# Two decodings of w_in put behind the row maxima on VectorE

## The chip, the cores and the metric

The kernel runs on one core of a Trainium2 chip. A core has five engines that share one on-chip memory and synchronise by semaphores: TensorE (PE, matmuls and transposes), VectorE (DVE), ScalarE (ACT), GpSimd (POOL) and SyncE (SP, which issues nearly all DMA transfers of this kernel). Each engine takes its instructions strictly in the order in which they stand in its own list. The metric is the device time of one execution in microseconds (us). Before the change it is 562.74 us, the median of 3 runs (561.09 to 566.05).

## What is computed

```python
# attention with decay, 4 batches x 8 heads, 576 tokens, head size 64
scores = q @ k.T / 8 + (cum[:, None] - cum[None, :])    # cum: running sum of log f; causal
attn   = softmax(scores);  y = attn @ v                 # -> x: 2304 x 512
# a gated layer
h = x @ w_in                                            # 512 x 2048
x = (h * sigmoid(1.702 * h)) @ w_out                    # 2048 x 512
# soft mixture of 8 experts with 4 slots each
logits = x @ phi                                        # 2304 x 32
slots  = softmax(logits, over tokens).T @ x             # 32 x 512
slots  = relu(slots @ w1[e]) @ w2[e]                    # 8 experts, 512 x 1024 x 512
out    = softmax(logits, over slots) @ slots            # 2304 x 512
```

`w_in` and `w_out` arrive as 64-bit floating point numbers. No engine computes in that format, so the kernel builds the 32-bit value of each element out of the two 32-bit halves of its words. That is the decoding that the change moves.

## The kernel before

**Attention.** The 2304 tokens are taken in 20 rows of up to 128 tokens, five for each batch (the fifth has 64). `prep_row` splits a row's queries and keys into a coarse and a fine 16-bit part and brings them into transposed form: for rows 0 to 2 by PE transposes whose results DVE and ACT copy out of PSUM, from row 3 on by transposing DMAs on SP's queue. For rows 1 to 4 the subtraction that makes the fine part stands on POOL (L325, L329), else on DVE. For rows 0 to 4 the row maximum is found ahead of the exponentials: `emit_max` computes the scores a first time (tile `scm`, in PSUM) and reduces them on DVE (L387) into tile `mt`; row 1 has 4 such steps of two heads each (u = 0 to 3) and row 3 has 8 of one head. `emit_mrow` negates the maxima on DVE (L432), PE transposes them (`mT`, L436), and ACT writes them beside the queries (L445), so that the second computation of the scores (tile `scs`, L467 to L471) already has the maximum taken off. Then follow the exponential on ACT (L489) and the product with the values on PE (`pv`, L623). `scm` and `scs` share 3 PSUM buffers: a new one is written only when DVE or ACT has read an old one.

**Decoding w_in.** It has 16 tiles of 128x512. Tile n is decoded in `w_first` in four steps: the word that holds sign, exponent and upper digits is scaled (L208 on POOL for even n, L210 on ACT for odd n), the lower word is converted into tile `low` (L211, ACT), and two DVE instructions join them with shifts and masks (L213 writes `low`, the **first half** below; L216 writes the tile, the **second half**). `low` has 2 buffers; one becomes free when a second half has read it. Then `split_one` makes a coarse part on ACT (L277) and a fine one on POOL (L278) for the matmuls `hp` (L800 to L802). Tiles 0 to 3 serve the first 512 columns of h, tiles 8 to 11 the third. `w_out` is decoded by the same lines later.

**Order.** The program is written in one sequence, in which `more_w` calls put the decoding between attention steps. A scheduler then places the instructions of each engine by its own forecast of when they can start, so that a line may stand earlier or later on its engine than in the program text. `tc.issue_after(x)` holds the instructions under it behind x on their engine; the kernel uses it already for some transposes of the gated layer.

**Later.** From about 46 us the gated layer's matmuls run between attention steps. When the last attention step is done its memory is given back, and the 127 loads of the experts' weights start (`we`, L1051), which the last part of the kernel works on.

Of the kernel before, what the change touches and what calls it, by code (L numbers as in the profile page):

```python
# [15 lines left out]
ALU = mybir.AluOpType  # L16
# [14 lines left out]
def attention_moe_softmoe(ctx, tc, q, k, v, f, w_in, w_out, phi, w1, w2, out):  # L31
    nc = tc.nc
# [28 lines left out]
    def ps_sc(name):  # L61
        return ps.tile([128, 512], F32, tag="sc", name=name, bufs=3)
# [106 lines left out]
    def w32_tile(n):  # L169
        if n < NI:  # L170
            return wp.tile([128, 512], F32, tag=f"w{n + 1}" if n < NI - 1 else "o0", name="w32")
        ff = n - NI
        if ff % 2 == 0:
            wo_pair[ff // 2] = wp.tile([128, 2, 512], F32, tag=f"o{ff // 2}", name="wo")
        return wo_pair[ff // 2][:, ff % 2]
# [21 lines left out]
    def w_first(n):  # L197


        if n in W32:  # L200
            nc.scalar.activation(out=W32[n], in_=W32[n], func=AF.Copy, scale=WS)
            return
        words = w_raw.pop(n).rearrange("p (n w) -> p n w", w=2)
        lo, hi = words[:, :, 0], words[:, :, 1]
        val = W32[n] = w32_tile(n)
        low = ap_.tile([128, 512], U32, tag="low", name="low", bufs=N_LOW)
        if n % 2 < 1:
            nc.gpsimd.tensor_scalar(out=val, in0=hi.bitcast(F32), scalar1=2.0 ** -111, scalar2=None, op0=ALU.mult)  # L208
        else:
            nc.scalar.activation(out=val, in_=hi.bitcast(F32), func=AF.Copy, scale=2.0 ** -111)  # L210
        nc.scalar.activation(out=low, in_=lo, func=AF.Copy, scale=0.93 * 2.0 ** -29)  # L211
        bits = val.bitcast(U32)
        nc.vector.scalar_tensor_tensor(  # L213
            out=low, in0=bits, scalar=3, in1=low, op0=ALU.logical_shift_left, op1=ALU.bitwise_or
        )
        nc.vector.scalar_tensor_tensor(  # L216
            out=bits, in0=bits, scalar=0x80000000, in1=low, op0=ALU.bitwise_and, op1=ALU.bitwise_or
        )

    def more_w(to):  # L220
        while w_at[0] < min(NW, to):
            n = w_at[0]
            w_at[0] += 1
            while w_loaded[0] < min(NW, n + W_AHEAD):
                w_load(w_loaded[0])
                w_loaded[0] += 1
            w_first(n)
            if n < NI:
                split_one(n)
            else:  # L230
                WO[n - NI] = W32.pop(n)
                if w_phi:
                    fold_phi(*w_phi.pop())
                w_phi.append((n - NI,))
        if w_at[0] == NW and w_phi:
            fold_phi(*w_phi.pop())
# [129 lines left out]
    def mask_in(o, m):  # L366
        nc.vector.tensor_tensor(out=o, in0=o, in1=m.unsqueeze(1).to_broadcast(list(o.shape)), op=ALU.add)

    def emit_max(r, u):
        b, i = rows[r]  # L370
        base = ROW[b, 0]
        m = mt[r % 2]
        if rows_of[i] == 128:
            hb = max(1, 4 // (i + 1))
            nb = 128 * (i + 1)
            sc = ps_sc("scm")
            for hh in range(hb):
                h = u * hb + hh
                for j in range(i + 1):
                    o = sc[:, hh * nb + 128 * j:hh * nb + 128 * (j + 1)]  # L380
                    mask = j == i and r < 5
                    nc.tensor.matmul(o, lhsT=QA[r][:, h, :], rhs=KA[base + j][:, h, :], start=True, stop=not mask)
                    if mask:
                        nc.tensor.matmul(o, lhsT=identb, rhs=mqk, start=False, stop=True)
            if r >= 5:
                mask_in(sc[:, 0:hb * nb].rearrange("p (h n) -> p h n", h=hb)[:, :, 128 * i:], mqk)
            nc.vector.tensor_reduce(  # L387
                out=m[:, 96 + u * hb:96 + (u + 1) * hb],
                in_=sc[:, 0:hb * nb].rearrange("p (h n) -> p h n", h=hb), axis=AX.X, op=ALU.max,
            )  # L390
        else:

            n = rows_of[i]
            sc = ps_sc("scm")
            if u < H // 2:
                for j in range(i):
                    for a in range(2):
                        nc.tensor.matmul(
                            sc[64 * a:64 * a + n, 128 * j:128 * (j + 1)], lhsT=QA[r][:, 2 * u + a, 0:n],
                            rhs=KA[base + j][:, 2 * u + a, :], start=True, stop=True,  # L400
                        )
                nc.vector.tensor_reduce(
                    out=m4[:, u], in_=sc[:, 0:128 * i], axis=AX.X, op=ALU.max
                )
            else:
                mask = r < 5
                for u in range(H // 2):
                    for a in range(2):
                        o = sc[64 * a:64 * a + n, n * u:n * (u + 1)]
                        nc.tensor.matmul(  # L410
                            o, lhsT=QA[r][:, 2 * u + a, 0:n], rhs=KA[r][:, 2 * u + a, 0:n], start=True, stop=not mask
                        )
                        if mask:
                            nc.tensor.matmul(o, lhsT=identb[:, 0:n], rhs=mqk[:, 0:n], start=False, stop=True)
                sv = sc[:, 0:n * (H // 2)].rearrange("p (h n) -> p h n", n=n)
                if not mask:
                    for a in range(2):
                        mask_in(sv[64 * a:64 * a + n], mqk[64 * a:64 * a + n, 64 * a:64 * a + n])
                m2 = ap_.tile([128, H // 2, 1], F32, tag="m2", name="m2", bufs=2)
                nc.vector.tensor_reduce(out=m2, in_=sv, axis=AX.X, op=ALU.max)  # L420
                nc.vector.tensor_tensor(out=m4, in0=m4, in1=m2, op=ALU.max)
# [228 lines left out]
    for pair in range(B // 2):  # L650
# [4 lines left out]
        n = rows_of[-1]  # L655
# [22 lines left out]
    def attn_items():  # L678
# [12 lines left out]
        for r in range(len(rows)):  # L691
# [27 lines left out]
            if r >= 1 and not late(r):  # L719
                n_m = n_max(r)  # L720
                hi = b0 - 1.5
                lo = max(preps.get(r, 0.0) + 0.5, hi - 0.9 * n_m)
                hi = max(hi, lo + 0.3)
                for m in range(n_m):
                    add(lo + (hi - lo) * (m + 0.5) / n_m, CM, emit_max, r, m)
                add(max(hi, b0 - 2), CR, emit_mrow, r)
# [337 lines left out]
    if True:  # L1064
# [6 lines left out]
        for u in range(n_max(0)):  # L1071
            emit_max(0, u)
# [18 lines left out]
        n = 0  # L1091
# [10 lines left out]
        for c in range(NCH):  # L1102
            t0, t1 = goals[c], goals[c + 1]
            NSTEP = 2 * N_UNIT
            n = 0
# [59 lines left out]
        for hf in range(2):  # L1165
            hsb[hf] = G[NCH - 1, 1, "ab"[hf]].rearrange("p a n -> p (a n)")
            for n in range(2):
# [9 lines left out]
                if done:  # L1177
                    turn(*done[-1])
                nc.scalar.activation(
                    out=hsb[hf][:, n * 512:(n + 1) * 512], in_=l1, func=AF.Relu, scale=zi[:, hf:hf + 1]  # L1180
# [21 lines left out]
        for p, (c0, c1) in enumerate(PARTS):  # L1202
            w = c1 - c0
            nr = 2
            for fb in range(WHOLE - KE, KE):
# [15 lines left out]
                out=s4[64:128], in0=p4[64:128], scalar=SS, in1=s4[64:128], op0=ALU.mult, op1=ALU.subtract  # L1221
# [13 lines left out]
            for k, blks in enumerate(groups):  # L1235
# [10 lines left out]
                if len(blk_tok[blks[0]]) == 1:  # L1246
                    tok = blk_tok[blks[0]][0][2]
                    queue.dma_start(
                        out=out[tok:tok + 128 * m, c0:c1].rearrange("(t p) n -> p t n", p=128), in_=ob
# [37 lines left out]
```

## Time and profile before

| | before |
|---|---|
| median of 3 runs | 562.74 us (561.09 to 566.05) |
| the profiled execution | 562.1 us, of which the span of its trace 560.4 us |
| mean granted TensorE clock | 0.973 of full speed |
| PE busy | 506.8 us (90%) |
| DVE busy | 354.5 us (63%) |
| ACT busy | 309.2 us (55%) |
| POOL busy | 69.0 us (12%) |

The span runs from the first to the last instruction of the profiled execution; 1.7 us of that execution lie outside of it. A share of busy time is an average over stages: POOL does nearly all of its work in the first 126 us, and DVE is far busier there than later. The time that an engine was idle before an instruction is put down to whatever released that instruction last. Register and semaphore work isn't counted as busy.

### The profile page before, as it was taken

What the parts mean: (1) busy time and instruction counts of PE and PEld (TensorE: products, weight loads), DVE (VectorE), ACT (ScalarE), POOL (GpSimd) and SP (SyncE); (2) the same over time, 40 slices, a digit from 0 to 9 for tenths busy, and PEclk for the clock granted to TensorE, in tenths of its full rate; (3) what the DMA queues carried; (4) which work ended last, traced back from release to release, by engine and by line L of the source; (5) the groups of instructions that cost most, each with busy time, mean ns of one, the idle gap of its engine ahead of it and who ended that gap; (6) DMA issues with size and microseconds to landing.
All of it is one profiled execution on the core that took longest, in us unless ns stands there. A gap on an engine that the chain in (4) does not pass through costs nothing.

```text
span 560.4 us, 13652 instructions
## 1 busy us (share of the span) xinstructions
PE 506.8 (90%) x5387; PEld 317.4 (57%) x5387; DVE 354.5 (63%) x934; ACT 309.2 (55%) x604; POOL 69.0 (12%) x120
## 2 busy tenths in 40 slices
PE   3566999998989999999999799989999999899991
PEld 3455876775666555665665466546566545454431
DVE  8988969787667357577776667866764413352022
ACT  6767786786767354565666566756564233312111
POOL 4866743310000000000000000000000000000000
PEclk9879799998999999999999899999999999999997
DMA  9997674999867227996759979995544199999999
GB/s 241 275 363 173 171 126 151 262 183 190 153 130 121 58 39 146 181 182 99 130 99 151 154 139 155 208 163 104 85 78 79 37 344 369 363 341 338 379 294 284
DMA packets 229823, 105.63 MB, mean 188 GB/s; under 512 B 202592, under 2 KB 211296, under 8 KB 229760
## 3 DMA queue, kind: packets, MB, share of 16 engines
q1 hardware_dynamic: 228528, 103.59, 80.0%
q10 hardware_dynamic: 1232, 1.18, 0.7%
q8 instruction: 42, 0.69, 0.5%
q14 instruction: 21, 0.17, 0.1%
HBM read 64.63 MB, written 4.72 MB: 124 GB/s over the span
## 4 chain that ended last, share of the span: by engine, by line
PE 70%; DMA 12%; DVE 8%; ACT 5%; issue 2%; SPq 2%; ACTq 0%; DVEq 0%
PE hp L800 10%; PE hp L801 9%; PE hp L802 9%; DMA ph<-pn 6%; PE gT L756 5%; PE p L778 4%; PE pv L623 3%; PE pv L628 3%; PE l L1172 3%; PE sp L921 2%; DMA kf<-in_k_dram 2%; PE scs L551 2%; DMA we<-in_moe_w_dram 2%; PE scs L552 2%; PE pv L630 2%
## 5 line engine op out<-in xcount | busy, mean ns | idle before, releaser
L800 PE MATMUL hp<-w,xt 128*128 128x512 f16 x288 | 110.4, 383 | 0.3 <-DVE spart L928 0.3
L801 PE MATMUL hp<-w,xt 128*128 128x512 f16 x288 | 109.8, 381 | 0.0
L802 PE MATMUL hp<-w,xt 128*128 128x512 f16 x288 | 109.7, 381 | 0.0
L578 ACT ACTIVATE pf<-scs,mx 128x512 f32<-128x512 f32 (+3 forms) x108 | 57.6, 541 | 40.9 <-DVE mx L574 31.7
L814 DVE SCALAR_TENSOR_TENSOR g<-g,hp 128x512 f32<-128x512 f32 x72 | 49.2, 683 | 41.6 <-ACT g L813 40.9
L813 ACT ACTIVATE g<-hp 128x512 f32<-128x512 f32 x72 | 42.6, 591 | 51.6 <-PE hp L802 46.4
L587 DVE SCALAR_TENSOR_TENSOR pn<-pf,pn 128x512 f16<-128x512 f32 (+2 forms) x78 | 51.0, 657 | 31.0 <-ACT pn L586 30.4
L586 ACT ACTIVATE pn<-pf 128x512 f16<-128x512 f32 (+2 forms) x78 | 47.0, 606 | 26.3 <-DMA ph<-pn 25.0
L628 PE MATMUL pv<-vv,ph 128*128 128x65 f16 (+2 forms) x360 | 45.9, 199 | 7.9 <-DMA ph<-pn 7.7
L574 DVE CUSTOM_DVE_ANT_0 scs<-scs,zmq 128x128 f32<-128x128 f32 (+3 forms) x96 | 46.6, 495 | 9.1 <-PE scs L552 6.9
L802 PEld LDWEIGHTS <-xt 128*128 128x128 f16 x288 | 28.3, 98 | 33.3 <-issue 0.6
L763 ACT COPY gt<-gT 128x512 f32<-128x512 f32 x71 | 41.1, 583 | 9.7 <-PE gT L756 9.3
L628 PEld LDWEIGHTS <-ph 128*128 128x128 f16 (+2 forms) x360 | 34.4, 102 | 20.0 <-DMA ph<-pn 10.2
L629 PE MATMUL pv<-vv,ph 128*128 128x65 f16 (+2 forms) x360 | 45.3, 196 | 0.0
L756 PE MATMUL gT<-ident,g 128*128 128x128 f32 x288 | 45.1, 277 | 0.0
L630 PE MATMUL pv<-vv,ph 128*128 128x65 f16 (+2 forms) x360 | 45.1, 195 | 0.0
L800 PEld LDWEIGHTS <-xt 128*128 128x128 f16 x288 | 28.8, 100 | 27.8 <-issue 4.7
L756 PEld LDWEIGHTS gT<-ident,g 128*128 128x128 f32 x288 | 33.9, 142 | 14.4 <-issue 5.0
L801 PEld LDWEIGHTS <-xt 128*128 128x128 f16 x288 | 28.3, 98 | 22.7 <-issue 0.7
L629 PEld LDWEIGHTS <-ph 128*128 128x128 f16 (+2 forms) x360 | 34.7, 103 | 1.9 <-issue 0.2
L551 PE MATMUL scs<-kab,qa 128*128 128x128 f16 x240 | 35.2, 220 | 0.4 <-ACT pf L578 0.4
L585 POOL MEMSET pn<- 128x128 f16 x12 | 2.5, 210 | 267.3 <-DMA ph<-pn 165.8
(226 smaller groups left out, 1036.3 us busy)
## 6 DMA issues: line engine op xcount, KB each, us to landing
we<-in_moe_w_dram SPq DMA_DIRECT2D x127, 256.0 KB, 5.6
raw<-in_moe_w_in_dram SPq DMA_DIRECT2D x16, 512.0 KB, 7.3
raw<-in_moe_w_out_dram SPq DMA_DIRECT2D x16, 512.0 KB, 6.0
kf<-in_k_dram SPq DMA_DIRECT2D x13, 256.0 KB, 3.7
qf<-in_q_dram SPq DMA_DIRECT2D x13, 256.0 KB, 4.1
vf<-in_v_dram SPq DMA_DIRECT2D x12, 256.0 KB, 4.4
out_dram<-ob SPq DMA_DIRECT2D x12, 256.0 KB, 3.2
ph<-pn SPq DMA_TRANSPOSE x78, 3.3
```

The costliest lines, as they stand in the source:

```text
L574: nc.vector.tensor_tensor_reduce(out=o, in0=o, in1=mask, scale=-SC, scalar=3.0e38 if n == 128 else DG[r][1][:, u], op0=ALU.add, op1=ALU.mi ...
L578: nc.scalar.activation(out=pf[:, hh * nb:(hh + 1) * nb], in_=o, func=AF.Exp, bias=mx[:, hh:hh + 1], scale=-1.0)
L586: nc.scalar.activation(out=pn[:, 0, 0:w], in_=pf, func=AF.Copy, scale=PB)
L587: nc.vector.scalar_tensor_tensor(out=pn[:, 1, 0:w], in0=pf, scalar=PB, in1=pn[:, 0, 0:w], op0=ALU.mult, op1=ALU.subtract)
L628: nc.tensor.matmul(o, lhsT=ph[0:rr, 0, off:off + n], rhs=vh, start=(j == 0), stop=False)
L629: nc.tensor.matmul(o, lhsT=ph[0:rr, 0, off:off + n], rhs=vl, start=False, stop=False)
L630: nc.tensor.matmul(o, lhsT=ph[0:rr, 1, off:off + n], rhs=vh, start=False, stop=(j == i))
L756: last_turn[0] = nc.tensor.transpose((pt if a < 2 else pt2)[:, a * 128:(a + 1) * 128], g[:, a * 128:(a + 1) * 128], ident)
L800: nc.tensor.matmul(hp, lhsT=xt[:, 0, kk, ts], rhs=win(0, fg, kk), start=(kk == 0), stop=False)
L801: nc.tensor.matmul(hp, lhsT=xt[:, 0, kk, ts], rhs=win(1, fg, kk), start=False, stop=False)
L802: last_hp[0] = nc.tensor.matmul(hp, lhsT=xt[:, 1, kk, ts], rhs=win(0, fg, kk), start=False, stop=(kk == KD - 1))
L814: nc.vector.scalar_tensor_tensor(out=g, in0=g, scalar=1.0, in1=hp, op0=ALU.add, op1=ALU.mult)
```

## The change

The first half of tile 2 is held behind the maximum (row 1, u = 3) on DVE, and the first half of tile 9 behind the maximum (row 3, u = 1). `maxima` keeps the reductions by row and step, so that they can be named. No instruction is added or taken away.

```diff
         bits = val.bitcast(U32)
-        nc.vector.scalar_tensor_tensor(
-            out=low, in0=bits, scalar=3, in1=low, op0=ALU.logical_shift_left, op1=ALU.bitwise_or
-        )
+        with tc.issue_after(maxima[BEHIND[n]].ins) if n in BEHIND else nullcontext():
+            nc.vector.scalar_tensor_tensor(
+                out=low, in0=bits, scalar=3, in1=low, op0=ALU.logical_shift_left, op1=ALU.bitwise_or
+            )
...
+    maxima = {}
+    BEHIND = {2: (1, 3), 9: (3, 1)}
...
-            nc.vector.tensor_reduce(
+            maxima[r, u] = nc.vector.tensor_reduce(
```

Since four lines are added, later lines of the changed kernel have higher numbers: L213 and L216 become L214 and L217, and from L217 on four are added (L387 becomes L391, L432 becomes L436).

**DVE, around row 1's maxima.** `w_222`, `w_233`, `w_371`, `w_405`, `w_500`, `w_545` are tiles 0 to 5 of w_in; `mt_84` holds the maxima of row 1. Before:

```order
L216 SCALAR_TENSOR_TENSOR w_233<-w_233,low 128x512
L213 SCALAR_TENSOR_TENSOR low<-w_371,low 128x512
L387 TENSOR_REDUCE mt_84<-scm 128x2 x2
L216 SCALAR_TENSOR_TENSOR w_371<-w_371,low 128x512
L213 SCALAR_TENSOR_TENSOR low<-w_405,low 128x512
L387 TENSOR_REDUCE mt_84<-scm 128x2
L216 SCALAR_TENSOR_TENSOR w_405<-w_405,low 128x512
L637 TENSOR_SCALAR rd<-pv 128x4
L213 SCALAR_TENSOR_TENSOR low<-w_500,low 128x512
L387 TENSOR_REDUCE mt_84<-scm 128x2
...
L213 SCALAR_TENSOR_TENSOR low<-w_545,low 128x512
L432 TENSOR_SCALAR mt_84<-mt_84 128x8
```

And now:

```order
L217 SCALAR_TENSOR_TENSOR w_233<-w_233,low 128x512
L391 TENSOR_REDUCE mt_84<-scm 128x2 x2
L214 SCALAR_TENSOR_TENSOR low<-w_405,low 128x512
L391 TENSOR_REDUCE mt_84<-scm 128x2
L217 SCALAR_TENSOR_TENSOR w_405<-w_405,low 128x512
L391 TENSOR_REDUCE mt_84<-scm 128x2
L214 SCALAR_TENSOR_TENSOR low<-w_371,low 128x512
L436 TENSOR_SCALAR mt_84<-mt_84 128x8
L641 TENSOR_SCALAR rd<-pv 128x4
L214 SCALAR_TENSOR_TENSOR low<-w_500,low 128x512
L217 SCALAR_TENSOR_TENSOR w_371<-w_371,low 128x512
```

Tile 2 stands behind the four maxima. Tile 3, which isn't held, has moved ahead of it, between the maxima. Three halves stand between tile 1 and the negation where seven stood.

**DVE, around row 3's first maxima.** `w_849`, `w_936`, `w_947`, `w_958`, `w_969` are tiles 7 to 11; `mt_83` holds the maxima of row 2 and `mt_84` those of row 3. Before:

```order
L432 TENSOR_SCALAR mt_83<-mt_83 128x8
L213 SCALAR_TENSOR_TENSOR low<-w_849,low 128x512
...
L216 SCALAR_TENSOR_TENSOR w_936<-w_936,low 128x512
L213 SCALAR_TENSOR_TENSOR low<-w_947,low 128x512
L814 SCALAR_TENSOR_TENSOR g<-g,hp 128x512
L637 TENSOR_SCALAR rd<-pv 128x4
L216 SCALAR_TENSOR_TENSOR w_947<-w_947,low 128x512
L213 SCALAR_TENSOR_TENSOR low<-w_958,low 128x512
...
L216 SCALAR_TENSOR_TENSOR w_969<-w_969,low 128x512
L323 COPY kan<-cpart 64x8x3
L387 TENSOR_REDUCE mt_84<-scm 128x1 x2
```

And now:

```order
L214 SCALAR_TENSOR_TENSOR low<-w_849,low 128x512
L436 TENSOR_SCALAR mt_83<-mt_83 128x8
...
L217 SCALAR_TENSOR_TENSOR w_936<-w_936,low 128x512
L641 TENSOR_SCALAR rd<-pv 128x4
L214 SCALAR_TENSOR_TENSOR low<-w_958,low 128x512
...
L214 SCALAR_TENSOR_TENSOR low<-w_969,low 128x512
L217 SCALAR_TENSOR_TENSOR w_969<-w_969,low 128x512
L391 TENSOR_REDUCE mt_84<-scm 128x1 x2
L214 SCALAR_TENSOR_TENSOR low<-w_947,low 128x512
```

Tile 9 stands behind row 3's first two maxima; tiles 10 and 11 still stand ahead of them. A half of tile 7 has moved ahead of row 2's negation.

**ACT, from row 1's negation to row 2's queries.** `qa<-mT` is the copy of the negated maxima, `qbn<-kqf` the coarse part of row 2's queries. Before:

```order
L211 ACTIVATE low<-raw 128x512
L277 ACTIVATE w<-w_371 128x512
L211 ACTIVATE low<-raw 128x512
L318 ACTIVATE kbn<-kqf 128x8x64
L489 ACTIVATE pf<-scs 128x512
L211 ACTIVATE low<-raw 128x512
L321 ACTIVATE qbn<-kqf 128x8x64
L277 ACTIVATE w<-w_405 128x512
L445 ACTIVATE qa<-mT 8x1024
```

And now:

```order
L211 ACTIVATE low<-raw 128x512
L322 ACTIVATE kbn<-kqf 128x8x64
L493 ACTIVATE pf<-scs 128x512
L449 ACTIVATE qa<-mT 8x1024
L281 ACTIVATE w<-w_371 128x512
L211 ACTIVATE low<-raw 128x512 x2
L325 ACTIVATE qbn<-kqf 128x8x64
L281 ACTIVATE w<-w_405 128x512
```

The copy of the maxima has moved ahead of tile 2's split, two conversions and row 2's queries. Behind these places the scheduler's order differs on every engine to the end of the attention; PE's own order is the same past the second group of `hp` matmuls, up to row 3's last maxima, but for one group of four `pv` products.

## Rows read from the trace of the kernel before

**Rows 1.** The page: busy tenths and granted clock in 40 slices of 14 us.

```profile
PE   3566999998989999999999799989999999899991
DVE  8988969787667357577776667866764413352022
PEclk9879799998999999999999899999999999999997
```

**Rows 2.** Timeline of PE: start us, duration us, what; in brackets the idle time before.

```profile
30.47 0.46 PE L436 MATMUL mT<-ident,mt 128*104 128x128 f32 x1 [6.85 <-DVE mt L432]
...
33.69 1.06 PE L340 MATMUL kqT<-ident,qbn 128*128 128x128 f16 x8
...
50.69 0.22 PE L384 MATMUL scm<-zmq,identb 128*128 128x128 bf16 x1
56.46 0.27 PE L467 MATMUL scs<-qa,kab 128*128 128x128 f16 x1 [5.55 <-DVE mt L387]
```

**Rows 3.** Windows of PE: from:to, length, busy us (count), granted clock, DMA.

```profile
35.00:36.50 1.50, 1.50 (x21) 0.94 0.99 322
...
54.50:56.00 1.50, 0.00 (x0) 0.88 0.67 268
...
62.00:63.50 1.50, 1.50 (x11) 0.84 0.76 147
```

**Rows 4.** Timeline of DVE around the maxima of rows 1 and 3.

```profile
18.76 0.69 DVE L216 SCALAR_TENSOR_TENSOR w<-w,low 128x512 uint32<-128x512 uint32 x1
...
22.74 1.64 DVE L213 SCALAR_TENSOR_TENSOR low<-w,low 128x512 uint32<-128x512 uint32 x1
24.31 0.68 DVE L387 TENSOR_REDUCE mt<-scm 128x2 f32<-128x512 f32 x1
24.91 0.68 DVE L216 SCALAR_TENSOR_TENSOR w<-w,low 128x512 uint32<-128x512 uint32 x1
...
29.30 1.12 DVE L432 TENSOR_SCALAR mt<-mt 128x8 f32<-128x8 f32 x1
...
45.69 0.17 DVE L432 TENSOR_SCALAR mt<-mt 128x8 f32<-128x8 f32 x1
...
49.78 1.20 DVE L213 SCALAR_TENSOR_TENSOR low<-w,low 128x512 uint32<-128x512 uint32 x1 [1.12 <-ACT low L211]
...
51.50 0.15 DVE L637 TENSOR_SCALAR rd<-pv 128x4 f32<-128x4 f32 x1
...
55.73 1.27 DVE L387 TENSOR_REDUCE mt<-scm 128x1 f32<-128x512 f32 x2
...
57.29 3.35 DVE L328 COPY qan<-qbn 64x512 f16<-64x512 f16 x1
```

**Rows 5.** Timeline of POOL beside the two long DVE instructions.

```profile
22.37 1.46 POOL L278 TENSOR_TENSOR w<-w,w 128x512 f16<-128x512 f32 x1
...
57.04 1.20 POOL L325 TENSOR_TENSOR kbn<-kf,kbn 64x512 f16<-64x512 f32 x1
58.21 1.14 POOL L329 TENSOR_TENSOR qbn<-qf,qbn 64x512 f16<-64x512 f32 x1
59.32 1.14 POOL L278 TENSOR_TENSOR w<-w,w 128x512 f16<-128x512 f32 x1
```

**Rows 6.** Windows: busy us (count) of PE, PEld, DVE, ACT, POOL; clock, DMA.

```profile
14.00:98.00 84.00, 65.69 (x647) 52.92 (x644) 74.96 (x135) 60.27 (x105) 51.30 (x42) 0.90 0.78 210
98.00:448.00 350.00, 338.29 (x3771) 212.03 (x3769) 236.30 (x681) 214.25 (x433) 10.84 (x45) 0.99 0.76 133
448.00:504.00 56.00, 53.92 (x432) 27.80 (x434) 19.61 (x60) 15.57 (x36) 0.68 (x1) 1.00 1.00 356
```

**Rows 7.** Timeline of SP's queue: the first stretch of the expert loads.

```profile
445.77 23.89 SPq L1051 DMA_DIRECT2D we<-in_moe_w_dram  x35
```

**Rows 8.** Timeline of PE and ACT: a later `hp`, and row 2's queries.

```profile
84.58 0.38 PE L800 MATMUL hp<-w,xt 128*128 128x512 f16 x1
...
28.41 0.62 ACT L321 ACTIVATE qbn<-kqf 128x512 f16<-128x512 f32 x1
```

## Prediction

> **What bounds the kernel now.** I began with the slices [rows 1]. PE is at 9 tenths nearly everywhere from the fifth slice on, so past 56 us a microsecond is won only by starting PE's work earlier. Before that PE stands at 5 and 6 tenths while DVE is at 8 and 9, and the granted clock dips in the third and fifth slice. The windows say it in sums [rows 6]: from 14 to 98 us PE works 65.7 of 84 us and DVE 75.0; from 98 to 448 us PE leaves only 11.7 of 350 us unused. So DVE bounds the start, and PE the rest up to 448 us. The end hangs on the same clock: the first of the experts' loads goes out at 445.77 us, when the last attention step has given its memory back [rows 7], and from then on the DMA engines are at 1.00 [rows 6]. What comes after that point keeps its length, so a gain that lasts until 446 us counts in full at the end.
>
> Then PE's timeline [rows 2]. Two idle stretches stand out: 6.85 us until row 1's negated maxima come (30.47), and 5.55 us until row 3's first maximum frees a PSUM buffer (56.46). These are the two places that the change touches. After each the clock is at half for a while [rows 3]: the window at 35.0 still has 0.94; the one at 54.5 has 0.88, which puts the fall at about 55.6, and the one at 62.0 has 0.84, which puts the return at about 62.5. PE thus worked at half speed from 56.46 to 62.5, 6.0 us that full speed would do in 3.0.
>
> Last DVE's own timeline [rows 4]. A maximum and a decoding half follow each other at 0.60 us (24.31 to 24.91). Some take longer because POOL is at work: the half at 22.74 lasts 1.64 beside a POOL subtraction from 22.37 to 23.83 [rows 4, 5], which is 0.96 over the usual 0.68; the negation at 29.30 takes 1.12 for eight columns.
>
> **The change part by part.** Nothing is added or removed; DVE has the same instructions in another order.
>
> Row 1. Tile 1's second half ends at 18.76 + 0.69 = 19.45, the negation at 29.30 + 1.12 = 30.42 [rows 4]. In the new order four maxima and three halves stand between, 7 x 0.60 = 4.2, then 0.15 for the negation, and I allow two waits of 0.96 for POOL: 19.45 + 4.2 + 0.15 + 1.9 = 25.7. The maxima reach PE 4.7 us earlier.
>
> Most of this is taken back at once. The decoding halves that stood ahead of the negation now stand behind it, and row 2 waits behind them. ACT takes row 2's `qbn` only behind tile 2's split and two `low` conversions, and the second of these needs a `low` buffer that a second half on DVE gives back. On DVE three halves follow the negation, 1.8 us, and with small ones of 0.2 and one POOL wait of 0.96 they end at 25.7 + 3.0 = 28.7. Add a conversion and `qbn`, 0.62 each like the `qbn` at 28.41 [rows 8], and a POOL subtraction of 1.2, behind another of 1.2 that is already under way: PE gets row 2's `qbn` at about 32.0, against 33.69 [rows 2]. Up to row 2's last copies DVE has executed the same instructions in both orders, and its waits for POOL I count at the same level. So of the 1.7 us I take **1.0**; bounds 0 (DVE's sum decides alone) and 4.7 (nothing is taken back).
>
> Row 3. From the negation of row 2 at 45.69 to the first maximum at 55.73 DVE needed 10.0 us with ten halves in between [rows 4]. Now the two halves of tile 9 are gone from there (1.2 us); a third has only moved in front of the negation, where it costs what it saves. The wait of 1.12 at 49.78, for tile 9's `low`, goes as well. That would be 2.3. But `rd` (51.50) now stands ahead of tiles 10 and 11, and it needs row 1's last `pv` products, which PE delivers near 49 to 50; the queue behind it waits up to 1.4 us. I take **0.9**, bounds 0 and 2.3. The change names tile 9 alone, and four halves of tiles 10 and 11 stay in front of the maximum: most of the 5.55 us of idle time stays.
>
> The clock. PE would run dry at about 50 and resume at 54.5, 4.4 us against 5.55. Before, the clock fell 4.7 us after PE ran dry (55.6 less 50.9) and came back 6.0 us after it resumed. The shorter gap can avoid the fall or halve it. I take **1.5** of the 3.0 us; bounds 0 and 3.0.
>
> Moved at no cost. Tile 2 is split later, but with tiles 0 to 3 it is needed by an `hp` that comes only after 46 us, some 16 us behind. Tile 9 is needed at 84.58 [rows 8], 27 us behind; if that cover went, each tile would cost PE up to the 2 x 0.60 of its halves and 1.2 for its split. SP's loads of w_in wait for ACT and POOL to have read the old raw tile, and those conversions move by 1 to 2 us at most. Where DVE's wait at 57.29 goes is not a term: PE did not stall there, but it covers the clock term, since a faster PE needs row 3's other maxima earlier. Behind 60 us the scheduler's order differs everywhere. I price it at 0, since PE is the bound there; bounds 4.0 either way, a third of the 11.7 us that PE leaves unused [rows 6].
>
> Sum: 1.0 + 0.9 + 1.5 = 3.4 us, from the profiled execution's 562.1 (span 560.4 and 1.7 around it) 558.7. The median of the runs stands 0.6 above that execution, so I say **559 us**.
>
> **One rule against a row.** The copy at 57.29 lasted 3.35 us, and it ended when a third POOL instruction in a row had ended (59.32 + 1.14 = 60.46) [rows 4, 5]; it had begun during the first. So on this chip DVE can wait through several.
>
> The Trainium skill (SBUF — State Buffer, section "SBUF: two separate sides") calls the port pair that DVE and GpSimd share an exclusive lock, held for the whole instruction by whoever starts first. By that rule as I read it the copy should have had its turn after the first one, at 58.24, with a wait of some 0.95; the row shows three times as much. The rule would make the third rival below cost 1.9 instead of 6.1.
>
> **The rivals.**
>
> *The idle time goes altogether* (24 in 100). If the reorder lets DVE run without its POOL waits and row 2 isn't held up, both gaps close and the clock stays up. DVE's own idle time between 14 and 98 us is 9.0 us [rows 6], and PE can't be fed faster than DVE works, so 9 us is what it can give: 553. For it speaks that the two gaps add up to 12.4; against it that the halves only change places.
>
> *The change does not do what it says* (16 in 100). The scheduler has put tile 3 between row 1's maxima, and tiles 10 and 11 ahead of row 3's. If the DVE sum up to row 2's copies is all that counts, and the clock falls as before, the kernel takes 562.
>
> *POOL starves DVE* (10 in 100), slower. Tile 4's split now follows row 3's `qbn` subtraction, and row 3's `kbn` and tile 5's split come next, so POOL may work without a pause while DVE wants to copy row 3's `qan` and `kan` for its DMA transposes. A run of three held DVE for 3.35 - 0.29 = 3.06 us at 57.29 (0.29 being such a copy when free). Two such waits on row 3's path cost 6.1, and they eat the first two gains: 562.1 + 6.1 = 568. It decides as soon as POOL has no gap at DVE's copies of row 3 near 36 to 39 us; before, there was one.
>
> **How the numbers follow.** The forecast as worked out has 50 in 100, with 554 to 564.5 as its own range (its terms at their bounds and a part of the 4.0). About 1% of the time, 5.6 us, is what a measurement of this kernel can tell from no change. Faster by over 1% means under 557.1: most of the first rival and some 16 of the forecast's 50, together 0.38. Slower by over 1% means over 568.4: half of the third rival and a little for the order behind 60 us, 0.08. The rest, 0.54, is within 1%. For 8 in 10 the range must take in most of the first rival and stop short of the third: 552 to 565.
>
> **What would show it.** Right: row 1's negation ends near 26 and PE's first idle stretch is split in two, the second part in front of row 2's transposes; row 3's first maximum starts near 54; PE's second idle stretch is 4 to 5 us; the first `we` load goes out near 442. Wrong: row 2's transposes near 29 (nothing was taken back); row 3's maxima not earlier than 55; the clock at half until 62 again; a POOL run with a DVE copy of 2 us or more beside it near 36 us; or a first `we` load that has moved by another amount than PE's work at 62 us, which would put the difference into the order behind it.

## The result, and the profile after

The change makes the kernel slightly slower: 567.08 us (562.26 to 570.41, 22 runs) against 563.01 (560.89 to 569.47, 22 runs) on the same chip, ratio 1.0054 [1.0032, 1.0075], which is 3.0 us [1.8, 4.2]. Here and below the figure in front is a median, and the bracket behind a ratio is its 95% interval; a ratio isn't the quotient of the two medians, which here differ by 4.1 us. Ratios are over executions within 1.5% of their kernel's fastest, which keeps all 44 of these but leaves out three of the 12 of run 6 below (567.57 to 568.59 us), so that its ratio may be too small. A gain of 3.4 was forecast. The profiled execution took 567.4 us, its span 565.7.

The windows answer to [rows 6], with the same columns: PE, PEld, DVE, ACT, POOL, clock, DMA.

```profile
14.00:98.00 84.00, 65.75 (x648) 52.94 (x645) 71.98 (x135) 60.42 (x105) 51.40 (x42) 0.90 0.76 214
98.00:448.00 350.00, 334.79 (x3734) 209.69 (x3732) 232.92 (x672) 212.38 (x432) 10.77 (x45) 0.99 0.76 131
448.00:504.00 56.00, 53.92 (x389) 27.18 (x384) 18.02 (x55) 16.65 (x38) 0.00 (x0) 1.00 0.95 339
```

In the first, which holds both changed places, PE works the same 65.7 us as before. In the second PE leaves 15.2 us unused instead of 11.7: 3.5 us more, in a stretch that the prediction held to be full. SP's queue shows the sum of it where [rows 7] had 445.77:

```profile
451.29 18.39 SPq L1055 DMA_DIRECT2D we<-in_moe_w_dram  x28
```

What follows this point lasts 114.4 us, before 114.6. So the tail kept its length, as forecast, and the loss lies ahead of it.

**The two places.** PE's timeline, answering to [rows 2]:

```profile
25.13 0.32 PE L440 MATMUL mT<-ident,mt 128*104 128x128 f32 x1 [2.22 <-DVE rd L641]
...
28.52 1.94 PE L627 MATMUL pv<-vv,pf 128*128 128x65 f32 x8 [3.07 <-ACT low L211]
...
31.35 1.03 PE L344 MATMUL kqT<-ident,qbn 128*128 128x128 f16 x8
...
39.19 0.22 PE L471 MATMUL scs<-qa,kab 128*128 128x128 f16 x1 [2.09 <-DVE mt L391]
...
56.65 0.27 PE L471 MATMUL scs<-qa,kab 128*128 128x128 f16 x1 [5.30 <-DVE mt L391]
```

The first idle stretch of 6.85 us became two, 2.22 and 3.07. The second went from 5.55 to 5.30. Between them the wait for a buffer that row 2's maxima give back (39.19) grew from 1.33 to 2.09. DVE's timeline, answering to [rows 4]:

```profile
24.79 0.28 DVE L436 TENSOR_SCALAR mt<-mt 128x8 f32<-128x8 f32 x1
...
45.84 0.68 DVE L214 SCALAR_TENSOR_TENSOR low<-w,low 128x512 uint32<-128x512 uint32 x1
46.43 0.17 DVE L436 TENSOR_SCALAR mt<-mt 128x8 f32<-128x8 f32 x1
...
50.44 0.16 DVE L641 TENSOR_SCALAR rd<-pv 128x4 f32<-128x4 f32 x1 [1.87 <-PE pv L627]
50.52 1.15 DVE L214 SCALAR_TENSOR_TENSOR low<-w,low 128x512 uint32<-128x512 uint32 x1
...
52.25 1.60 DVE L217 SCALAR_TENSOR_TENSOR w<-w,low 128x512 uint32<-128x512 uint32 x1
...
55.91 1.28 DVE L391 TENSOR_REDUCE mt<-scm 128x1 f32<-128x512 f32 x2
...
58.63 0.28 DVE L332 COPY qan<-qbn 64x512 f16<-64x512 f16 x1
```

Row 1's negation comes 4.5 us earlier (24.79 against 29.30). Row 2's comes 0.74 later (46.43 against 45.69): the advantage has gone within one row. Row 3's first maximum starts at 55.91, against 55.73.

Part of that loss goes with the clock, which fell a further time just after PE's wait of 2.09 us. Windows of the changed kernel, of the kernel before, and of run 5 below, which has the changed kernel's order up to 138 us:

```profile
40.50:43.50 3.00, 3.00 (x21) 2.94 (x20) 1.54 (x4) 2.26 (x5) 2.36 (x2) 0.50 1.17 218
```
```profile
40.50:43.50 3.00, 2.86 (x36) 2.69 (x36) 2.58 (x6) 1.44 (x3) 2.66 (x3) 1.00 1.16 194
```
```profile
40.50:43.50 3.00, 3.00 (x38) 2.88 (x39) 2.60 (x7) 2.95 (x6) 2.01 (x2) 1.00 1.32 219
```

In run 5, whose clock stayed up, row 2's negation and row 3's first maximum come earlier than before:

```profile
45.23 0.43 DVE L436 TENSOR_SCALAR mt<-mt 128x8 f32<-128x8 f32 x1
...
55.00 1.28 DVE L391 TENSOR_REDUCE mt<-scm 128x1 f32<-128x512 f32 x2
```

Run 1 below has the fall and the changed kernel's times (46.42 and 55.90), run 7 has neither (45.26 and 55.01). In these four traces of one order the fall thus goes with 1.2 us at the negation and 0.9 at the maximum. Why the clock fell in two of them and not in the others isn't shown.

The clock around the second idle stretch, as windows of PE (busy of PE, PEld, DVE, ACT, POOL; granted clock, DMA), answering to [rows 3]:

```profile
52.50:54.00 1.50, 0.00 (x0) 0.00 (x0) 1.50 (x2) 0.12 (x1) 0.80 (x1) 1.00 0.94 207
...
54.50:56.00 1.50, 0.00 (x0) 0.00 (x0) 1.39 (x3) 0.94 (x3) 0.49 (x1) 0.50 0.88 358
...
60.50:62.00 1.50, 1.50 (x15) 1.26 (x13) 0.35 (x1) 1.10 (x3) 1.50 (x2) 0.88 0.56 87
62.00:63.50 1.50, 1.50 (x13) 0.79 (x11) 1.16 (x2) 1.03 (x2) 1.50 (x2) 1.00 0.68 123
```

It is full up to 54, half after that (1.2 of 2.4 GHz), and back within the window at 60.5: a mean of 0.88 means half for a quarter of it, so the return is at about 60.9. From 56.65 on PE thus works 4.2 us at half speed, where it was 6.0. That saves 0.9. The stretch at half speed is as long as before (54.0 to 60.9, against 55.6 to 62.5); it only came 1.6 us earlier, so that more of it fell on PE's idle time. Why it came earlier isn't shown: PE ran dry 0.4 us later than before (51.35 against 50.91).

**Behind 62 us.** One sort of milestone runs through both traces: the steps of the gelu (L813, now L817) on ACT, each released by PE's last `hp` of a piece. The ninth and fourteenth after the first, and the one at 396 us, of before:

```profile
142.54 0.60 ACT L813 ACTIVATE g<-hp 128x512 f32<-128x512 f32 x1 [0.66 <-PE hp L802]
...
184.34 0.59 ACT L813 ACTIVATE g<-hp 128x512 f32<-128x512 f32 x1
...
396.36 0.58 ACT L813 ACTIVATE g<-hp 128x512 f32<-128x512 f32 x1
```

and after:

```profile
141.36 0.59 ACT L817 ACTIVATE g<-hp 128x512 f32<-128x512 f32 x1
...
189.77 0.58 ACT L817 ACTIVATE g<-hp 128x512 f32<-128x512 f32 x1
...
401.87 0.58 ACT L817 ACTIVATE g<-hp 128x512 f32<-128x512 f32 x1
```

The changed kernel is 1.2 us ahead at 142 us, 5.4 behind at 184 and 5.5 behind at 396, after which both have the same order. Between these PE takes some work in another order, so not every step compares like with like: at the one at 291.21 of before it is 3.2 behind (294.38). PE's two long waits between the first pair are these:

```profile
146.23 1.06 PE L273 MATMUL wps<-rsum,part 128*128 128x32 f32 x4 [1.79 <-ACT part L262]
...
161.48 0.20 PE L632 MATMUL pv<-vv,ph 128*128 128x65 f16 x1 [1.90 <-DMA ph<-pn]
```

The first is a queue: `part` stands on ACT behind row preparation (`kbn`), and that waits 1.87 us for its load `kf`. The second waits for a transposing DMA. Neither waits for a tile of w_in. Behind each wait the clock is at half for a while. Windows of the changed kernel, then one of before:

```profile
146.50:149.50 3.00, 3.00 (x10) 1.50 (x11) 2.56 (x6) 1.21 (x3) 0.00 (x0) 0.50 0.97 97
...
163.50:166.50 3.00, 3.00 (x8) 1.06 (x7) 0.56 (x1) 0.92 (x2) 0.00 (x0) 0.50 0.40 79
```
```profile
134.50:137.50 3.00, 3.00 (x35) 2.23 (x34) 1.51 (x5) 2.31 (x6) 0.00 (x0) 0.50 1.62 175
```

PE works throughout the first two windows, so at full clock it would have needed 1.5 us less in each. Before, the clock was full from 142 to 172 us, but had been at half just ahead, which is about what the changed kernel's lead of 1.2 us at 142 is made of. The difference of two single traces in this stretch is thus in good part where the clock fell.

### The profile page after: what moved, and what is told of

Its sections match the earlier page's. It is cut to its first block, busy times and chain, and to the rows that moved or that the text cites. A ratio compares the mean times of both kernels' runs of the same rounds, so it can differ in the third digit from the quotient of the medians.

```text
span 565.7 us, 13649 instructions
## 1 busy us (share of the span) xinstructions
PE 509.1 (90%) x5387; PEld 317.9 (56%) x5387; DVE 350.4 (62%) x934; ACT 308.7 (55%) x604; POOL 69.1 (12%) x120
## 4 chain that ended last, share of the span: by engine, by line
PE 62%; DMA 15%; DVE 8%; ACT 6%; issue 4%; SPq 2%; POOL 1%; ACTq 0%; DVEq 0%; POOLq 0%
PE hp L804 10%; PE hp L805 9%; PE hp L806 9%; DMA ph<-pn 6%; PE gT L760 5%; PE p L782 4%; DMA we<-in_moe_w_dram 3%; PE pv L632 3%; PE sp L925 2%; PE l L1176 2%; DMA kab<-kan 2%; PE scs L555 2%; PE scs L556 2%; PE pv L627 2%; PE pv L634 2%
## 5 line engine op out<-in xcount | busy, mean ns | idle before, releaser
L817 ACT ACTIVATE g<-hp 128x512 f32<-128x512 f32 x72 | 42.5, 590 | 52.4 <-PE hp L806 47.3
```

## The experiments

All instructions have the same names in both kernels, and only their order differs. So an order can be forced by a table: each instruction of an engine is put behind the one ahead of it in the table, over the whole program. With that, the order of one kernel can be grafted on the other. The table by itself costs nothing that shows: run 8 has one and takes the time of the kernel before. Ratios are to the kernel before on the same chip; 0.001 is 0.56 us.

```diff
         attention_moe_softmoe(tc, *args)
+        _force(tc)
```

**1. New order to 62 us, order of before behind it** (the change itself, and `_force`).

> The changed kernel's order on every engine up to about 62 us (past row 3's first two maxima and tile 9's decoding), and from there the order of the kernel before, laid down by a table. Theory A (the held halves cost nothing lasting; the 5.5 us were lost because the scheduler put the instructions behind 62 us in another order): within 1 us of the kernel before, 561 to 563, and the first load of the experts' weights goes out near 446 us. Theory B (the held halves themselves cost: row 2 and what follows come late, and the loss surfaces later): 566 to 568, first load near 451.

Measured: 1.0013 [0.9982, 1.0044], that is 0.7 us longer [-1.0, 2.5]: theory A's time. The forecast 3.4 us of gain at the two places is outside. (In the one trace the loads start at 444.05, 1.7 us earlier than before; the executions as a whole don't show that.)

**2. Order of before to 62 us, new order behind it** (no half held, and `_force` with the other table).

> The mirror image: the order of the kernel before up to about 62 us, and from there the order of the changed kernel, laid down by a table; no half is held. Theory A: as slow as the changed kernel, 566 to 568, first load of the experts' weights near 451 us. Theory B: like the kernel before, 561 to 563, first load near 446.

Measured: 1.0047 [1.0016, 1.0077], 2.6 us [0.9, 4.3]. The median, 564.51, and the first load, 447.10, lie between the two theories. The two parts add up to 1.006, the change gives 1.0054. So, by the middle values, most of the loss comes from a part of the order in which none of the moved halves stands; the intervals of the two parts overlap.

**3 and 4. One half alone**, the scheduler free.

```diff
-    BEHIND = {2: (1, 3), 9: (3, 1)}
+    BEHIND = {2: (1, 3)}
```

> Only tile 2 is held behind row 1's last maximum; the scheduler places all the rest. Both theories: row 1's negation ends near 25 us as in the changed kernel. Theory A: the total depends on the order that the scheduler makes of the rest, 560 to 568, and isn't half of the change's cost. Theory B: it carries the larger part of the cost, 564 to 566.

> Only tile 9 is held behind row 3's second maximum. Both theories: row 1 as in the kernel before (negation ends near 30.4 us), row 3's first maximum 1 to 2 us earlier than 55.7. Theory A: the total depends on the order of the rest, 560 to 568. Theory B: 563 to 564, the smaller part of the cost.

Measured: 1.0099 [1.0059, 1.0138] for tile 2, 1.0092 [1.0057, 1.0128] for tile 9 (`BEHIND = {9: (3, 1)}`). The intervals overlap with the change's, but the two don't add up to it: a cost that belonged to the two places would come to some 1.019 for both together, and 1.0054 was measured. One that comes from whatever order the scheduler then finds can do that. The signs were half right: with tile 2 alone row 1's negation ends at 25.63, but with tile 9 alone row 3's first maximum isn't earlier (55.78 against 55.73), since DVE waits 1.75 us for ACT's gelu where the halves of tile 9 stood.

**5 to 7. Where behind 62 us, and through which queue.** Run 5 has the new order up to about 138 us, run 6 only from 138 to 227 us, both with the order of before elsewhere.

> Both halves held; the changed kernel's order on every engine up to about 138 us, the order of before from there on, by a table. In the trace of the changed kernel PE was 1.2 us ahead of before at the gelu step at 142.5 us and 5.4 us behind at the one at 184 us, so theory A (the loss arises between 138 and 227 us) expects 559.5 to 562 us, ratio 0.997 to 1.001. Rival B (the new order costs in proportion to its length from 62 to 395 us, 2.6 us in all by the two grafts) expects a quarter of that, about 562.5 us, ratio 1.002 to 1.003.

> No half held; the order of before up to about 138 us and from about 227 us on, the changed kernel's order between them. Theory A expects the whole loss: 564 to 566 us, ratio 1.004 to 1.008, with the transposes ph<-pn or ACT's wait for kf ahead of PE's idle time there. Rival B expects a quarter, ratio 1.001 to 1.002. If it is below 1.001, the loss needs a different state of the queues at 138 us and can't be tied to this stretch alone.

Measured: 1.0060 [1.0031, 1.0088] and 1.0048 [1.0014, 1.0082]. The second agrees with a loss between 138 and 227 us, the first contradicts it: it should have been without loss, and it is longer than the rival had it, too. Both pieces cost about as much as the whole.

The traces don't settle it. Run 5's is of one of its quicker executions (561.55 us, where the median is 564.42), and in it the loads start at 445.36, 0.4 us earlier than before; so where the other executions lose their time isn't in it. PE's busy time from 138 to 196 us is 55.88 us before, 53.55 after the change (at a clock of 0.94), 52.00 in run 2 and 53.03 in run 5, but also 53.90 in run 9 below, which isn't slower. Nor do the gelu steps tell: run 9 has the order of before throughout, and in its trace a lead of 3.2 us at the step at 142.54 has become 0.4 behind at the one at 291.21. So what is shown is that grafting this stretch costs 2.7 us (run 6), and that the order in it isn't the whole cause (run 5). That the state in which the queues reach it counts too is argued, not shown.

Run 7 keeps the changed kernel's order on PE, DVE, ACT and POOL, and gives SP the order of before from 138 us on.

> The changed kernel's order on PE, DVE, ACT and POOL throughout, but SP issues its transposes and loads from about 138 us on in the order of before, in which the transposes qa and qb of the next row stand one ph transpose earlier. If SP's order alone makes the loss (theory A1), PE's idle time between 140 and 168 us shrinks and the time is 562 to 564 us, ratio 0.999 to 1.003. If ACT's and PE's orders make it (A2), the time stays at 566 to 568 us, ratio 1.005 or more.

Measured: 572.88 us, 1.0218 [1.0192, 1.0245], 12.2 us. Neither theory had that. SP's timeline in the changed kernel, from 138 us on, and then in this run:

```profile
143.05 2.87 SPq L595 DMA_TRANSPOSE ph<-pn  x2
...
149.84 16.47 SPq L595 DMA_TRANSPOSE ph<-pn  x7
169.19 1.20 SPq L350 DMA_TRANSPOSE qa<-qan  x1
```
```profile
148.81 14.09 SPq L595 DMA_TRANSPOSE ph<-pn  x6
167.47 1.20 SPq L350 DMA_TRANSPOSE qa<-qan  x1
168.75 1.22 SPq L350 DMA_TRANSPOSE qb<-qbn  x1
170.03 0.58 SPq L310 DMA_DIRECT2D kf<-in_k_dram  x1
...
173.04 3.34 SPq L595 DMA_TRANSPOSE ph<-pn  x2
```

Between one row's `qa` and the next there are nine `ph` transposes in the first, and eight in the second (two of them ahead of the rows shown). What ACT, DVE and PE waited for in this run:

```profile
177.23 0.52 ACT L590 ACTIVATE pn<-pf 128x384 f16<-128x384 f32 x1 [8.40 <-DMA ph<-pn]
```
```profile
177.78 0.56 DVE L591 SCALAR_TENSOR_TENSOR pn<-pf,pn 128x384 f16<-128x384 f32 x1 [8.67 <-ACT pn L590]
```
```profile
178.73 1.22 PE L857 MATMUL lg<-l,rsum 128*128 128x256 f32 x2 [5.73 <-DVE l L849]
```

So a `ph` transpose stands on SP behind the next row's transposes and loads, at 173.04. ACT, in its own order, wants its next `pn` and waits 8.40 us for that transpose to give the buffer back; DVE waits 8.67 behind ACT, PE 5.73 behind DVE. One queue in an order that fits other neighbours took the kernel from 3.0 to 12.2 us behind before. How much of these 9.2 us is this one stall isn't shown; the spans of the two traces differ by 6.0. SP's order, then, is right or wrong only together with the other engines'.

**8. More halves held, order of before behind 62 us.** Tile 3 now stands behind row 1's last maximum like tile 2, and tiles 9, 10 and 11 all stand behind row 3's first two maxima.

```diff
-    BEHIND = {2: (1, 3), 9: (3, 1)}
+    BEHIND = {2: (1, 3), 3: (1, 3), 9: (3, 1), 10: (3, 1), 11: (3, 1)}
```

> More halves held: tiles 2 and 3 behind row 1's last maximum, tiles 9, 10 and 11 behind row 3's second; from about 62 us the order of before on every engine. Theory C (a half that is moved behind a maximum is waited for later, so its place is worth nothing) expects the time of before within 1 us, ratio 0.998 to 1.002. Rival D (the gain was missing because the scheduler filled the two places with tiles 3, 10 and 11) expects the four halves of tiles 10 and 11 and one or two of tile 3 off the path, 2.4 to 3.6 us: 558 to 559.5 us, ratio 0.993 to 0.996, with row 3's first maximum at 53 to 54 us.

Measured: 1.0007 [0.9986, 1.0027], 0.4 us longer [-0.8, 1.5]: theory C's time, and rival D's is outside. DVE's timeline:

```profile
49.74 1.27 DVE L391 TENSOR_REDUCE mt<-scm 128x1 f32<-128x512 f32 x2
50.94 2.33 DVE L214 SCALAR_TENSOR_TENSOR low<-w,low 128x512 uint32<-128x512 uint32 x2
...
68.27 0.17 DVE L436 TENSOR_SCALAR mt<-mt 128x8 f32<-128x8 f32 x1
```

Row 3's first maximum starts 6.0 us earlier than in [rows 4], but the halves now stand between this row's maxima, and its negation comes only 1.9 us earlier (70.20 before). PE, which had its stretch of 5.55 us taken away, waits 3.47 at 57.33 instead. In this trace 2.5 us are still left when the loads start (443.23 against 445.77); the executions as a whole don't show them.

**9 and 10. Halves made short.** Here work is taken away instead of moved: the two DVE halves of some tiles touch 16 of 512 columns, so most of these tiles isn't decoded. The order is that of before on every engine. Run 9 shortens tiles 9 to 11, run 10 tiles 2 to 11 (`2 <= n < 12`).

```diff
+        if 9 <= n < 12:
+            low, bits = low[:, 0:16], bits[:, 0:16]
         nc.vector.scalar_tensor_tensor(
```

> The order of before on every engine; both DVE halves of w_in's tiles 9, 10 and 11 work on 16 of 512 columns, so most of these tiles isn't decoded. Six halves of 0.60 us shrink to about 0.08: DVE has 3.1 us less to do ahead of row 3's first maximum. Theory P (PE is the bound behind 56 us, so time won at the start arrives at the end) expects 2.5 to 3.5 us less than before, ratio 0.994 to 0.996. Rival N (waits behind 62 us take it back) expects 0.998 to 1.002, with the gelu steps earlier by 2 us or more at 65 us and by less than 1 us at 400 us.

> As the run before, but with the halves of tiles 2 to 11 narrow: twenty halves, 10.4 us less work for DVE from 19 to 56 us. Theory P expects most of PE's two idle stretches to go and 7 to 10 us at the end, ratio 0.982 to 0.988. Rival N expects less than 2 us, ratio above 0.996.

Measured: for tiles 9 to 11, 0.9986 [0.9964, 1.0008], 0.8 us less [-0.4, 2.0] out of 3.1; for tiles 2 to 11, 0.9905 [0.9874, 0.9937], 5.3 us [3.5, 7.1] out of 10.4. The first is rival N's, the second lies between the two theories. By the middle values a quarter and a half of the time won on DVE arrives; the intervals allow up to two thirds. The gelu steps of the two traces show where the rest goes: the step at 65.18 of before comes 2.0 us earlier in run 9 and 6.0 in run 10, the one at 396.36 only 1.0 and 3.3. So a part is lost ahead of 65 us and a part behind. DVE's timeline in the first of the two shows the part ahead:

```profile
52.71 1.27 DVE L389 TENSOR_REDUCE mt<-scm 128x1 f32<-128x512 f32 x2
55.44 0.45 DVE L324 COPY kan<-kbn 64x512 f16<-64x512 f16 x1 [1.45 <-ACT kbn L320]
55.96 3.35 DVE L330 COPY qan<-qbn 64x512 f16<-64x512 f16 x1
...
68.53 0.91 DVE L434 TENSOR_SCALAR mt<-mt 128x8 f32<-128x8 f32 x1
```

The first maximum is 3.0 us earlier. Then DVE waits for ACT, and row 4's copy of `qan` takes 3.35 us beside POOL as in [rows 4]; row 3's negation is 1.7 us earlier. Its path runs over ACT's and POOL's splitting too, and not over DVE's halves alone.

**11. The halves of run 8, the scheduler free.**

> Tiles 2 and 3 held behind row 1's last maximum, 9 to 11 behind row 3's second, and no order by a table: the scheduler's own order behind 62 us. Theory A (any other order behind 62 us costs what the two grafts showed) expects 563.5 to 567 us, ratio 1.004 to 1.010. Its rival (the cost belongs to the one order of the changed kernel) expects the ratio of the run with the order of before behind 62 us, 0.998 to 1.003.

Measured: 571.37 us, 1.0161 [1.0118, 1.0204], 9.0 us: theory A's side, and more than it had. Runs 8 and 11 have the same order to about 62 us on PE, DVE, ACT and POOL (SP's transposes differ from 55 us on): 1.0007 against 1.0161. These 8.6 us are the clearest measure of what an order behind 62 us is worth, about three times what the whole change did. Not all of them need be the order's: in the two traces 2.2 us stand already at the second gelu step (61.65 and 63.84), and the last section shows what that can be. No kernel that computes everything was clearly faster than the one before.

## Why the prediction was wrong

**The steps that failed** are two, and the first is the larger. The three gains, 1.0 + 0.9 + 1.5 = 3.4 us, were to last to the end; measured by themselves (run 1) they came to -0.7 us [-2.5, 1.0], 4.1 less. And "Behind 60 us the scheduler's order differs everywhere. I price it at 0, since PE is the bound there": measured by itself (run 2) this is -2.6 us [-4.3, -0.9].

**The order behind 60 us** stayed within the bounds of 4.0 that were given, but it got the middle of its range. PE's share of 0.97 from 98 to 448 us is not a reason for 0: each of the four other orders that a scheduler made (the change, runs 3, 4 and 11) was slower than the kernel before, by 3.0 to 9.0 us, though for runs 3 and 4 nothing separates the part behind 62 us from the part ahead. Bounds that are symmetric around a well-fed PE are wrong where PE has little left to gain and much to lose. The prediction had named the sign of this, a first `we` load that moves by another amount than PE's work at 62 us, and it came: the gelu step at 65.18 is 0.7 us earlier, the load 5.5 later.

**The three gains.** The working at row 1 was right and that at row 3 was not, and what row 1 won didn't last:

| step | forecast | after |
|---|---|---|
| row 1's negation ends | 25.7 | 25.07 |
| first idle stretch splits | yes, the second part at row 2's transposes | yes, 2.22 and 3.07, the second at row 1's `pv` (28.52) |
| PE has row 2's `qbn` | 32.0 | 31.35 |
| row 3's first maximum starts | near 54 | 55.91 |
| second idle stretch | 4 to 5 | 5.30 |
| saved by the clock | 1.5 | 0.9 |
| first `we` load | 442 | 451.29 |

Row 1's term was taken at row 2's transposes, and there it stood, with 2.3 us (31.35 against 33.69). It was lost one step later: ahead of row 2's negation stands the half of tile 7 that "costs what it saves" (45.84, 0.6), and between row 2's maxima DVE now waits 1.87 us for PE in four pieces, where it waited 0.31. Of this 1.2 us go with the clock's fall at 40 us, a term that the sum didn't have.

Row 3's term was 0.9. From row 2's negation to row 3's first maximum DVE now needs 9.5 us where it needed 10.0, so 0.6 was won there, and the later negation took it back. The term had named the wait for `rd` (up to 1.4; 1.87 came) and not the two halves that POOL stretches to 1.15 and 1.60 beside it.

The clock's term was to come from a shorter gap that avoids the fall or halves it. The gap stayed (5.30 for 5.55), the half-speed stretch is as long as before, and the 0.9 comes from its earlier place: that is luck, and not the mechanism.

**The assumption behind all of them**, that what is won at the start lasts until 446 us and then counts in full, was never a row. Runs 9 and 10 give 0.8 of 3.1 and 5.3 of 10.4. By these shares even a right 3.4 us at the start would have been some 0.9 to 1.7 at the end, an estimate.

**The rivals.** That the idle time goes altogether did not happen: the two stretches of 12.4 us became 10.6 in three. POOL starving DVE near 36 to 39 us did not either: row 3's longest copies there took 1.17 and 1.13, no longer than before, although POOL had no gap there, as this rival asks, and the copy at 57.29 even lost its wait (58.63, 0.28). "The change does not do what it says" was nearest for the two places, where its 562, no change, is within run 1's interval; but run 8, which holds the tiles that had moved into the places, gave no more. No rival had the order behind 60 us as its mechanism. Its 4.0 stood in the text as a bound, and the only slower rival was POOL's.

**The rule against a row.** Run 9 repeats the row: the `qan` copy from 55.96 to 59.31 spans the rest of one POOL instruction and two whole ones (POOL at 55.70, 56.87 and 57.98, 1.20, 1.15 and 1.15 long). But the changed kernel has a copy beside POOL instructions that follow each other as closely, and it ended at 37.64, just after the first of them:

```profile
36.32 1.17 POOL L329 TENSOR_TENSOR kbn<-kf,kbn 128x512 f16<-128x512 f32 x1
37.44 1.20 POOL L282 TENSOR_TENSOR w<-w,w 128x512 f16<-128x512 f32 x1
```
```profile
36.47 1.17 DVE L326 COPY kan<-kbn 128x512 f16<-128x512 f16 x1
```

So the reading of the Trainium skill (SBUF — State Buffer, section "SBUF: two separate sides") by which a copy has its turn after the first is borne out here and not in run 9. What decides between the two isn't shown. Priced by the longer wait alone, the third rival was too dear.

**What stays open.** Which instruction behind 62 us starts the loss of 2.6 us: runs 5 and 6 don't agree on one stretch. Why the granted clock falls in one trace of an order and not in the next, at 40 us for one. And whether the 2.5 us that run 8's trace shows are real: the kernel before ran from 558.56 to 567.67 us in 29 executions, so two single traces can't settle it.

## What to carry to other kernels

Where a scheduler places the instructions, a change of two of them is a change of all that follow: before pricing the places, compare the whole order, and give the rest a range that leans to the slower side if the kernel is well tuned. Force the old order behind the changed place, and the two costs can be measured apart. An engine that is 97% busy is no proof that time won ahead of it arrives: shorten the disputed work and see how much does. Before two single traces are compared, compare where the clock fell in each.

## What the runs showed of the hardware

Runs 8 and 11 have one order up to about 55 us, and yet PE's mean granted clock from 28 to 42 us was 0.79 in the one trace and 0.53 in the other:

```profile
28.00:42.00 14.00, 11.43 (x117) 10.45 (x118) 13.59 (x23) 9.86 (x16) 11.32 (x10) 0.79 1.10 355
```
```profile
28.00:42.00 14.00, 11.37 (x88) 10.46 (x89) 11.96 (x20) 9.38 (x15) 9.99 (x8) 0.53 1.09 368
```

PE was busy for the same time and did 117 and 88 matmuls in it, and the first gelu step came at 47.69 and 49.95. So 2.3 us between two traces can be the clock alone. What kept it lower in run 11 isn't shown: PE had waited 2.27 us until 27.76 in run 8 and 2.55 us until 27.86 in run 11.
